# Prologue of a fused attention and feed-forward kernel: one denominator and one maximum operation, key-value transposes in the replica bank, and a reordered entry into the feed-forward steps

## The chip, the cores and the metric

The kernel runs on one core of one Trainium2 chip. The metric is the device time of one execution in microseconds (us). Five runs of the kernel before gave a median of 194.73 us, from 194.39 to 196.03.

The text uses the profile's names of the engines: PE is the matrix engine and PEld its weight loads, DVE the vector engine, ACT the scalar engine, POOL the GpSimd engine. SP is the engine that issues nearly all DMA transfers, in one queue and in program order. Each engine works through its own instructions in order, and semaphores hold an instruction until what it needs is there.

## The reference

The first half is attention with a polynomial feature map in place of the softmax, for batch 4, 4 heads, sequence 1088, head dimension 32. S1 and S2 are 8x32 matrices.

```python
def phi(x):
    a = np.einsum('rd,bhsd->bhsr', S1, x)
    b = np.einsum('rd,bhsd->bhsr', S2, x)
    return np.einsum('bhsi,bhsj->bhsij', a, b).reshape(*x.shape[:-1], r * r)
q_p, k_p = phi(q), phi(k)                        # 64 features
kv  = np.einsum('bhsf,bhsd->bhfd', k_p, v)
z   = np.sum(k_p, axis=2)
num = np.einsum('bhsf,bhfd->bhsd', q_p, kv)
den = np.einsum('bhsf,bhf->bhs', q_p, z)[..., None] + 1e-06
attn = num / den
```

The heads are then put side by side, which gives 4352 tokens of width 128, and the second half is a feed-forward layer on them: `h = max(x @ w_in, 0)`, then `out = (h * h) @ w_out`, with an inner width of 2048.

## The kernel before

**Tiling.** A batch has 1088 tokens. They are worked on in three chunks of 384, 384 and 320 tokens. The feed-forward layer of one chunk is 16 steps, one for each block of 128 inner columns. So there are 4 x 3 x 16 = 192 steps. A step is a first-layer matmul into `pg` (L908), a relu into `gt` by ACT (L918) or DVE (L920), a square into `g` by ACT (L902), DVE or POOL (L929), and a second-layer matmul that adds into `po` (L939). `ffn1(i)` records the first three, and `ffn2(i)` the last. The first layer runs three steps ahead (`LA = 3`). PSUM has two buffers for `pg`, so the first layer of step i+2 waits for the relu of step i.

**Prologue.** Before step 0 the attention of batch 0, chunk 0 must be there. Keys are turned on DVE (`a_kT`), PE makes their features `kf`, ACT and DVE build the products `kp`, and PE sums keys times values and keys alone over nine tiles of 128 tokens into `kvp` (L393, L407). The queries' features are made by three "replica" matmuls `rep` (L1087), each followed by a product on DVE (L1092). Two of the replicas stand in the two halves of `x0`, a PSUM tile of two banks in the pool slot named X. Then `nd` (L778) multiplies queries and sums into numerators and denominators in another tile, in the pool slot named N. `kvT` (L486) turns the sums for later chunks and writes into that same tile; `kw` (L498) copies the turned sums out.

The function `a_x1` takes denominators `den` (for chunk 0 by two ACT operations, L794) and row maxima `mx` (two DVE operations, L805, one for each bank), and a reciprocal `rden`. `a_x2` and `a_x3` scale the numerators to `xs` in 16 bits by a power of two that is taken off again after the layer. The squared power `beta` comes from two small DVE operations, `mp` and `beta` (L857, L861), at the end of `a_x3`. `a_xp` and `a_xT` turn `xs` into the layer's input `xT`. `keep_warm` runs matmuls on a tile of zeros while PE has nothing to do: `WARM0` of them at the start and `WARM` in front of step 0.

**What else runs beside the steps.** Chunk 1 of batch 0 (`old_chunk`) makes its query features on DVE by lane shuffles (`qb`, `qa`) and products (`qp`), and then needs an `nd` group of its own on PE. Chunk 2 makes them on PE (`a_qg`, L519) and DVE (`a_sh`). `br` holds `beta` spread over the partitions; `f_br` makes it by 16 small copies on POOL for each of the first two chunks, and `f_ob` multiplies a finished output chunk by it (L1003) before SP stores it (L1013). Batch 1 is prepared meanwhile: loads, `a_kT`, key features in a group with the `ndn` matmuls of chunk 2 (L550 with L431), their spreading `a_fs` (L352), the products `a_kp2` (L361, one half on DVE, one on POOL), and their sum over nine tiles, `a_kv9`. From batch 1 on, query features move between partitions by SP transfers, the `ft` moves (`a_mv`, L626).

**What sets the order.** The order is written out by the program. `_Plan` is a list of slots, one for each step. A task is added with its engine, a duration, the tasks that it needs and sometimes a first slot; it goes to the first slot in which that engine's planned load stays under a cap, one or two slots after what it needs. On POOL tasks take non-overlapping stretches. `balance()` then chooses for each step which engines do relu and square, from what the slots have left. The main loop records, for slot i, the first layer of step i+3, the second layer of step i and then that slot's tasks. DMA issues are in the plan too; in the program an issue on SP also waits for the landing of the DMA eight before it.

The entry into the steps is written by hand:

```python
    for cols in ((0, 128), (128, 384)):
        ffn1(0, ("ACT", "DVE"), cols)
    for i in range(1, LA):
        ffn1(i, ("ACT", ("DVE", "ACT")[i % 2]))
    a_qg(0, 2)
    for cols in ((0, 128), (128, 384)):
        ffn2(0, cols)
```

Of the kernel before, what the change touches and what calls it, by code (L numbers as in the profile page):

```python
# [73 lines left out]
def kernel(  # L74
# [26 lines left out]
    WARM0, WARM = 9, 7  # L101
# [61 lines left out]

    s_nat = cpool.tile([32, 32], F32)
# [3 lines left out]
    zero = cpool.tile([128, 512], F16)  # L168
    nc.vector.memset(zero[:], 0.0)  # L169
# [34 lines left out]
    load_qk(qn[0], q, 0, 384, 768)  # L204
    load_w_in(0, nc.sync)
    load_w_o(0)
    load_qk(qn[0], q, 0, 768, S)
# [20 lines left out]
    eps = cpool.tile([128, 1], F32)  # L228
    nc.gpsimd.memset(eps[:], 1e-6)
# [16 lines left out]
    def a_set(i):  # L246
        if i == 0:
            p_ = list(S2r.ap)[0][0]
            for g in range(2):
                nc.sync.dma_start(  # L250
                    bass.AP(S2r.tensor, S2r.offset + g * p_, [[2 * p_, 64], [1, 32]]),
                    bass.AP(S2.tensor, S2.offset, [[0, 8], [D, 8], [1, D]]),
                )
            nc.gpsimd.memset(sw[0][:], 0.0)
# [48 lines left out]
    for h in range(H):  # L303
        (nc.vector.tensor_copy if h < 2 else nc.scalar.copy)(
            _ap(sk, 32 * h, 32, 16 * h, [[1, 2], [2, 8]]),
            _ap(s_T, 0, 32, 0, [[8, 2], [1, 8]]),
        )
# [175 lines left out]
    def a_kvT(b):  # L483
        c0 = 768 if b == 0 else 512
        for i in range(2 if b == 0 else 1):
            nc.tensor.transpose(  # L486
                st[b, "N"][:, c0 + 128 * i : c0 + 128 * i + 128],
                st[b, "kvs"][:, 128 * i : 128 * i + 128],
                iden[:, :],
            )  # L490
        if b > 0:
            nc.tensor.matmul(st[b, "N"][:, 640:672], S2b[:, :], st[b, "gm"][:, :])

    def a_kw(b):

        n, c0 = (256, 768) if b == 0 else (128, 512)
        kw = st[b, "kw"] = wpool.tile([128, 256], F32, tag="kw", name="kw")
        nc.scalar.copy(kw[:, 0:n], st[b, "N"][:, c0 : c0 + n])  # L498
# [288 lines left out]
    def a_x1(b, ch):  # L787
# [4 lines left out]
        for g in range(2):  # L792
            if ch == 0:
                nc.scalar.activation(  # L794
                    _ap(den, 0, 128, 2 * g, [[4, 3], [1, 2]]),
                    _ap(nd, 0, 128, 512 * g + 32, [[66, 3], [33, 2]]), Iden, bias=eps[:, 0:1],
                )
        if ch > 0:
            nc.vector.tensor_scalar(
                out=_ap(den, 0, 128, 0, [[2, 2], [4, 3], [1, 2]]),  # L800
                in0=_ap(nd, 0, 128, 32, [[512, 2], [66, 3], [33, 2]]),
                scalar1=1e-6, scalar2=None, op0=add,
            )
        for g in (1, 0):
            nc.vector.tensor_reduce(  # L805
                out=_ap(mx, 0, 128, 2 * g, [[4, 3], [1, 2]]),
                in_=_ap(nd, 0, 128, 512 * g, [[66, 3], [33, 2], [1, 32]]),
                axis=AX, op=amax, apply_absolute_value=True,
            )
# [27 lines left out]
    def a_x3(b, ch, o=0, n=3):  # L837
# [17 lines left out]
        if o + n == 3:  # L855
            mp = wpool.tile([128, 3], F32, tag="mp", name="mp")
            nc.vector.tensor_scalar(  # L857
                out=mp[:, :].bitcast(U32), in0=mm[:, :].bitcast(U32),
                scalar1=EXP, scalar2=None, op0=band,
            )  # L860
            nc.vector.scalar_tensor_tensor(  # L861
                out=st[b, "beta"][:, 3 * ch : 3 * ch + 3], in0=mp[:, :], scalar=2.0**-20,
                in1=mp[:, :], op0=mult, op1=mult,
            )
# [194 lines left out]
    def keep_warm(n):  # L1059

        t_ = st["warm"]
        for _ in range(n):
            nc.tensor.matmul(t_[:, 0:512], zero[:, 0:128], zero[:, :])  # L1063
# [4 lines left out]
    a_fs(0, 0)  # L1068
    a_kf(0, 1, psf, "pg")
# [38 lines left out]
    for lo, n in ((0, 2), (2, 3)):  # L1108
# [6 lines left out]
    for t in range(4, NT):  # L1115
        st[0, "kp", t] = kp4, [256 * (t - 4) + 64 * h for h in range(H)]
    for t in range(4):
        a_kv(0, t)
        a_z(0, *st[0, "kp", t], False)
    x0 = psa.tile([128, 1024], F32, tag="X", name="rep")  # L1120
    replicated(0, x0[:, 0:512])
# [23 lines left out]
    products(1)  # L1145
    a_qT(0, 384, 768)
    a_kvs(0)
    a_nd(0, 0)
    a_kvT(0)
    a_qc(0, 1, psf, "po")  # L1150
# [12 lines left out]
    a_qb(0, 1)  # L1163
    a_qT(0, 768, S)
# [30 lines left out]
    def old_chunk():  # L1195

        b, ch = 0, 1
        P.at["qb", b, ch] = -1
        for e in range(E):
            P.add(("qa", b, ch, e), "DVE", 0.58, [("qb", b, ch)], a_qa, b, ch, e)  # L1200
# [5 lines left out]
        P.at["N"] = P.at["x3", b, ch]  # L1206
        P.add(("xd", b, ch), "SP", 0.0, [("x3", b, ch)], a_xd, b, ch)
# [60 lines left out]
    def x_tasks(b, ch):  # L1268
# [13 lines left out]
        if b == 0:  # L1282
            P.add(("xs", b, ch), "POOL", 0.95, [("rs", b, ch)], a_xs, b, ch)
# [3 lines left out]
        P.add(("bt", b, ch), "POOL", 1.0, [("s2", b, ch)], a_beta, b, ch)  # L1287
# [4 lines left out]
    def k_tasks(n):  # L1292
        for g in range(2):
# [7 lines left out]
        if n == 1:  # L1301
            x_tasks(0, 2)
# [27 lines left out]
    P.add(("kw", 0), "ACT", 0.4, [], a_kw, 0)  # L1330
    old_chunk()
    f_br(0, 0, 0, 1)
# [4 lines left out]
    P.add(("br", 0, 0), "POOL", 2.6, [], f_br, 0, 0, 1, 4)  # L1337
# [11 lines left out]
    P.add(("br", 0, 1), "POOL", 3.6, [("x3", 0, 1)], f_br, 0, 1)  # L1349
# [57 lines left out]
    for cols in ((0, 128), (128, 384)):  # L1407
        ffn1(0, ("ACT", "DVE"), cols)
    for i in range(1, LA):
        ffn1(i, ("ACT", ("DVE", "ACT")[i % 2]))  # L1410
    a_qg(0, 2)
    for cols in ((0, 128), (128, 384)):
        ffn2(0, cols)
# [49 lines left out]
```

## Time and profile before

| what | value |
|---|---|
| median of five runs | 194.73 us |
| the profiled execution, whole | 194.57 us |
| its span, first to last instruction | 192.8 us |
| PE busy | 184.5 us, 96% of the span |
| ACT, DVE, POOL busy | 68%, 61%, 47% of the span |
| first matmul of the feed-forward layer | starts at 16.90 us |
| first second-layer matmul | starts at 18.89 us |
| mean granted PE clock | 0.993 of full |

The profile is of one execution, and all its times count from the start of its span; some 1.8 us of the execution lie outside the span. A line of the profile gives a start or a total, a length, the engine, the line of the program and the operation with its tiles. "SPq" is SP's queue of issues. In the chain of waits, each piece is the work that the next one waited for, followed back from the last instruction. PE operations overlap their neighbours, so a matmul's own length is longer than the time from its start to the next one's.

### The profile page before, as it was taken

The page shows a single profiled execution, that of the slowest core. Times are in us where ns is not written, and L with a number is a line of the kernel's source. Part 1 is how long each engine was busy: PE and PEld are TensorE (multiplying, and loading weights), DVE is VectorE, ACT ScalarE, POOL GpSimd, SP SyncE. Part 2 cuts the span into 40 slices and gives each one's busy share as a digit, 9 for nine tenths or more (in the row PEclk, how much of TensorE's full clock was granted, in tenths as well). Part 3 has the DMA queues.
Part 4 walks back from the last instruction along what each step waited for, and adds up shares of the span by engine and source line. Part 5 has one row for each costly group of instructions (what it writes and reads, how often), then busy time and mean ns, then how long its engine had stood idle before and what let it go on. Part 6 is the DMA issues. An engine that isn't in the chain of part 4 may idle for free.

```text
span 192.8 us, 4421 instructions
## 1 busy us (share of the span) xinstructions
PE 184.5 (96%) x1540; PEld 110.1 (57%) x1540; DVE 118.5 (61%) x284; ACT 130.5 (68%) x322; POOL 90.4 (47%) x172
## 2 busy tenths in 40 slices
PE   7997999999999989999999999999999999999990
PEld 2673655474655456555556456555566555556990
DVE  3858995966739836466439764684382835637740
ACT  3316696956949848677769676587595966856840
POOL 5834465682447933334648941532666642250000
PEclk9999999999999999999999999999999999999997
DMA  5699406020143500341346201202304021200201
GB/s 164 155 299 318 91 20 236 0 44 0 40 93 87 169 10 24 66 119 35 69 96 180 60 0 37 51 2 58 47 12 85 12 58 27 41 0 2 44 0 36
DMA packets 30081, 13.93 MB, mean 72 GB/s; under 512 B 20202, under 2 KB 28778, under 8 KB 30058
## 3 DMA queue, kind: packets, MB, share of 16 engines
q1 hardware_dynamic: 29910, 13.58, 28.9%
q8 instruction: 12, 0.20, 0.4%
q14 instruction: 11, 0.09, 0.2%
q10 hardware_dynamic: 148, 0.07, 0.1%
HBM read 8.80 MB, written 2.23 MB: 57 GB/s over the span
## 4 chain that ended last, share of the span: by engine, by line
PE 81%; SPq 5%; DVE 5%; DMA 3%; issue 2%; ACT 1%; DVEq 0%; ACTq 0%
PE po L939 50%; PE pg L908 14%; PE kvp L393 3%; SPq L141 3%; PE ndn L637 2%; PE warm L1063 2%; PE pt L956 2%; DMA ft<-ft 2%; PE nd L778 2%; PE qk L564 1%; PE rep L1087 1%; SPq L626 1%; SPq L1013 1%; DMA ft<-u 1%; DVE kp L361 1%
## 5 line engine op out<-in xcount | busy, mean ns | idle before, releaser
L939 PE MATMUL po<-g,w_o 128*128 128x384 f32 (+3 forms) x386 | 144.1, 459 | 0.0
L918 ACT ACTIVATE gt<-pg 128x384 f32<-128x384 f32 (+2 forms) x139 | 65.3, 473 | 35.6 <-PE pg L908 35.0
L939 PEld LDWEIGHTS po<-g,w_o 128*128 128x128 f32 x386 | 65.6, 190 | 33.3 <-ACT g L902 16.9
L902 ACT ACTIVATE g<-gt 128x384 f32<-128x384 f32 (+1 forms) x146 | 72.2, 506 | 6.9 <-DVE gt L920 6.4
L908 PE MATMUL pg<-xT,w_in 128*128 128x384 f16 (+2 forms) x193 | 60.9, 317 | 0.7 <-ACT xT L880 0.3
L929 POOL TENSOR_TENSOR g<-gt 128x384 f32<-128x384 f32 (+1 forms) x44 | 34.8, 798 | 46.5 <-ACT gt L918 46.4
L920 DVE TENSOR_SCALAR gt<-pg 128x384 f32<-128x384 f32 (+1 forms) x54 | 28.8, 534 | 27.4 <-PE pg L908 20.0
L908 PEld LDWEIGHTS <-w_in 128*128 128x128 f16 x193 | 19.1, 99 | 22.1 <-issue 4.3
L599 POOL TENSOR_TENSOR qp<-tq,bs 128x384 f32<-128x384 f32 (+1 forms) x18 | 14.2, 811 | 16.1 <-DVE bs L591 16.1
L361 POOL TENSOR_TENSOR kp<-fs 128x384 f32<-128x384 f32 x9 | 13.2, 1488 | 1.3 <-DVE fs L352 1.3
L573 DVE STREAM_TRANSPOSE tq<-qk 128x384 f32<-128x384 f32 (+1 forms) x9 | 5.0, 561 | 13.0 <-PE qk L564 8.6
L738 POOL TENSOR_TENSOR bt<-s 128x384 f32<-128x384 f32 (+1 forms) x10 | 8.2, 815 | 7.1 <-DVE s L712 7.1
L971 POOL COPY br<-beta 32x3 f32<-32x3 f32 x32 | 5.8, 182 | 6.7 <-DVE beta L861 5.4
L985 DVE SCALAR_TENSOR_TENSOR sc<-po,bt 128x384 f32<-128x384 f32 (+1 forms) x9 | 4.8, 531 | 6.4 <-PE po L939 6.3
L361 DVE TENSOR_TENSOR kp<-fs 128x1152 f32<-128x1152 f32 x3 | 7.2, 2416 | 0.0
L720 DVE TENSOR_SCALAR rs<-ndn 128x384 uint32<-128x384 uint32 (+1 forms) x9 | 4.8, 536 | 3.6 <-PE ndn L704 3.5
L637 PE MATMUL ndn<-ft,kw 64*32 64x192 f32 (+1 forms) x144 | 6.4, 325 | 0.6 <-DMA ft<-u 0.6
L393 PEld LDWEIGHTS kvp<-kp,vn 128*32 128x32 f32 x288 | 5.4, 109 | 2.7 <-PE pg L908 1.1
L1063 PE MATMUL warm<-zero 128*128 128x512 f16 x16 | 5.7, 521 | 1.2 <-DVE zero L169 1.2
L325 DVE STREAM_TRANSPOSE qT<-qn 128x384 f32<-128x384 f32 (+1 forms) x12 | 6.5, 540 | 0.0
L393 PE MATMUL kvp<-kp,vn 128*32 128x64 f32 x288 | 6.5, 223 | 0.0
L637 PEld LDWEIGHTS ndn<-ft,kw 64*32 64x32 f32 x144 | 2.5, 104 | 5.9 <-PE pg L908 5.0
(147 smaller groups left out, 161.5 us busy)
## 6 DMA issues: line engine op xcount, KB each, us to landing
vn<-in_v_dram SPq DMA_DIRECT2D x32, 64.0 KB, 2.2
kn<-in_k_dram SPq DMA_DIRECT2D x3, 544.0 KB, 4.8
qn<-in_q_dram SPq DMA_DIRECT2D x3, 544.0 KB, 4.1
ft<-u SPq DMA_DIRECT2D x24, 48.0 KB, 1.9
out_dram<-oT SPq DMA_DIRECT2D x24, 48.0 KB, 1.8
w_in<-in_moe_w_in_dram SPq DMA_DIRECT2D x2, 512.0 KB, 7.3
w_o<-in_moe_w_out_dram SPq DMA_DIRECT2D x2, 512.0 KB, 8.6
ft<-ft SPq DMA_DIRECT2D x12, 48.0 KB, 2.0
```

Source lines behind the costliest of these rows:

```text
L361: (nc.vector if g == 0 else nc.gpsimd).tensor_tensor(out=_ap(st[b, "kp2"], 0, 128, 128 * (NT * g + lo), [[64, 2 * (hi - lo)], [8, 8], [1, ...
L393: nc.tensor.matmul(st[b, "kvp"][32 * h : 32 * h + 32, 0:64], _ap(vn[b], 0, n, v0 + dv * h, [[1, 32]]), kp[0:n, at[h] : at[h] + 64], start= ...
L599: nc.gpsimd.tensor_tensor(out=_ap(qp, 0, 128, 0, [[32, m], [8, 4], [1, 8]]), in0=_ap(st[b, "tq", ch], 0, 128, 4 * e, [[32, m], [1, 4], [0, ...
L637: nc.tensor.matmul(nd[32 * h : 32 * h + 32, 512 * g : 512 * g + n], st[b, "kw"][64 * g : 64 * g + 64, 32 * h : 32 * h + 32], st[b, ch, "ft ...
L738: nc.gpsimd.tensor_tensor(out=bt[:, 0:n], in0=st[b, "s2", ch][:, 0:n], in1=st[b, "s2", ch][:, 0:n], op=mult)
L902: nc.scalar.activation(dst, src, Square)
L908: nc.tensor.matmul(pg[:, c0:c1], w_in[:, 128 * c : 128 * c + 128], st[b, "xT"][:, 384 * ch + c0 : 384 * ch + c1],)
L918: nc.scalar.activation(gt[:, c0:c1], pg[:, c0:c1], Relu)
L920: nc.vector.tensor_scalar(out=gt[:, c0:c1], in0=pg[:, c0:c1], scalar1=0.0, scalar2=None, op0=amax)
L929: (nc.vector if on[1] == "DVE" else nc.gpsimd).tensor_tensor(out=g2[:, c0:c1], in0=gt[:, c0:c1], in1=gt[:, c0:c1], op=mult)
L939: nc.tensor.matmul(st["po", b, ch][:, c0:c1], w_o[:, 128 * c : 128 * c + 128], g2s[i][1][:, c0:c1], start=first, stop=(c == NFF - 1), skip ...
L1063: nc.tensor.matmul(t_[:, 0:512], zero[:, 0:128], zero[:, :])
```

## The change

- In `a_x1`, `den` is one DVE operation over both banks for chunk 0 too, and `mx` is one operation over both banks for both chunks. The two ACT operations and the tile `eps` are gone.
- `a_kvT` of batch 0 writes the turned sums into the first 256 columns of the replica tile `x0`, no longer into the tile of `nd`. `kw` follows at once on ACT, before the cast of the first half of `w_in`; it was a task of slot 0.
- `replicated(0, ...)` stands before the sums of the first four key tiles, no longer after them. `kp4` is made in parts of three and two tiles (it was two and three).
- The queries of batch 0 from column 384 on come in one load, no longer two, and both turns of them stand before `a_x1`.
- `mp` and `beta` become a function of their own, `a_bt`, planned in slot 1 for chunk 0 and behind `x3` for chunk 1.
- The entry: DVE and ACT take turns at relu and square from step 0's first part on, step 0's second layer starts before step 2's first layer, and `a_qg(0, 2)` stands behind step 2's first layer. `qb` of chunk 1 is a task of slot 0.
- `zero` has 128 columns, is filled first and is read four times over. `WARM` is 4, and one warm matmul stands between the two groups of `kf`. One copy of `sk` goes to ACT and one to POOL.
- The fills and sums of `sw` and `pr` on POOL become `a_set(2)` and stand before the steps.
- In the plan: `xs` and `bt` of chunk 2 on POOL get first slots 20 and 24; `br` of chunk 0 is one task of 16 copies that needs `bt`, in slot 6; `br` of chunk 1 gets first slot 20; `x_tasks(0, 2)` stands before the `fs` and `kp` tasks of batch 1.

As the plan comes out: the `nd` of chunk 1 goes from slot 3 to 4, the group of L550 and L431 from slot 10 to 11, POOL's `kp` of batch 1 from slots 12 to 14 to slots 15 to 17, `a_kv9` stays in slot 19, and `br` of chunk 1 goes from slot 20 to slot 30, behind `qp2` of batch 1. The POOL squares of steps 13 and 19 go to ACT; from slot 42 on the two plans are the same.

```diff
-    WARM0, WARM = 9, 7
+    WARM0, WARM = 9, 4
...
-    load_qk(qn[0], q, 0, 384, 768)
+    load_qk(qn[0], q, 0, 384, S)
     load_w_in(0, nc.sync)
     load_w_o(0)
-    load_qk(qn[0], q, 0, 768, S)
...
     def a_kvT(b):
-        c0 = 768 if b == 0 else 512
+        dst = st["kvT", b] = x0[:, 0:256] if b == 0 else st[b, "N"][:, 512:672]
...
-        for g in range(2):
-            if ch == 0:
-                nc.scalar.activation(
-                    _ap(den, 0, 128, 2 * g, [[4, 3], [1, 2]]),
-                    _ap(nd, 0, 128, 512 * g + 32, [[66, 3], [33, 2]]), Iden, bias=eps[:, 0:1],
-                )
-        if ch > 0:
-            nc.vector.tensor_scalar(
...
-        for g in (1, 0):
-            nc.vector.tensor_reduce(
-                out=_ap(mx, 0, 128, 2 * g, [[4, 3], [1, 2]]),
-                in_=_ap(nd, 0, 128, 512 * g, [[66, 3], [33, 2], [1, 32]]),
-                axis=AX, op=amax, apply_absolute_value=True,
-            )
+        nc.vector.tensor_scalar(
+            out=_ap(den, 0, 128, 0, [[2, 2], [4, 3], [1, 2]]),
+            in0=_ap(nd, 0, 128, 32, [[512, 2], [66, 3], [33, 2]]),
+            scalar1=1e-6, scalar2=None, op0=add,
+        )
+        nc.vector.tensor_reduce(
+            out=_ap(mx, 0, 128, 0, [[2, 2], [4, 3], [1, 2]]),
+            in_=_ap(nd, 0, 128, 0, [[512, 2], [66, 3], [33, 2], [1, 32]]),
+            axis=AX, op=amax, apply_absolute_value=True,
+        )
...
+    replicated(0, x0[:, 0:512])
     for t in range(4):
         a_kv(0, t)
         a_z(0, *st[0, "kp", t], False)
-    x0 = psa.tile([128, 1024], F32, tag="X", name="rep")
-    replicated(0, x0[:, 0:512])
...
+    a_set(2)
     a_qT(0, 384, 768)
+    a_qT(0, 768, S)
     a_kvs(0)
     a_nd(0, 0)
     a_kvT(0)
+    a_kw(0)
...
-    a_qb(0, 1)
-    a_qT(0, 768, S)
...
-    f_br(0, 0, 0, 1)
+    P.fix(("bt", 0, 0), "DVE", 0.35, 1, a_bt, 0, 0)
...
-    P.add(("br", 0, 0), "POOL", 2.6, [], f_br, 0, 0, 1, 4)
+    P.add(("br", 0, 0), "POOL", 3.6, [("bt", 0, 0)], f_br, 0, 0)
...
-    P.add(("br", 0, 1), "POOL", 3.6, [("x3", 0, 1)], f_br, 0, 1)
+    P.add(("br", 0, 1), "POOL", 3.6, [("bt", 0, 1)], f_br, 0, 1, first=20)
...
-    for cols in ((0, 128), (128, 384)):
-        ffn1(0, ("ACT", "DVE"), cols)
-    for i in range(1, LA):
-        ffn1(i, ("ACT", ("DVE", "ACT")[i % 2]))
+    ffn1(0, ("DVE", "ACT"), (0, 128))
+    square_due()
+    ffn1(0, ("ACT", "DVE"), (128, 384))
+    ffn1(1, ("DVE", "ACT"))
+    ffn2(0, (0, 128))
+    ffn1(2, ("ACT", "DVE"))
     a_qg(0, 2)
-    for cols in ((0, 128), (128, 384)):
-        ffn2(0, cols)
+    ffn2(0, (128, 384))
```

## The prediction

> **What bounds the kernel now.** First the shares, then the chain that ended last in order of time, then single instructions where that chain leaves the matmul engine. The page's shares:
>
> ```profile
> PE 184.5 (96%) x1540; PEld 110.1 (57%) x1540; DVE 118.5 (61%) x284; ACT 130.5 (68%) x322; POOL 90.4 (47%) x172
> ```
>
> PE is the bound. From 24 us on it repeats one step: 0.16 us first layer, 0.65 us second. So the change pays only by letting the steps start sooner, and loses where a later PE group waits. The chain of waits, each piece with start and length:
>
> ```profile
> 10.95 0.86 PE rep L1087 x2
> 11.88 1.56 PE nd L778 x24
> 13.44 0.38 PE nd L486 x2
> ...
> 13.91 0.43 ACT den L794 x2
> 14.37 0.62 DVE mx L805 x2
> 14.99 0.15 DVE rden L810
> ...
> 15.97 0.70 DVE xs L846 x3
> ...
> 17.46 0.28 PE pg L908
> 17.77 0.39 ACT gt L918
> 18.20 0.32 PE pg L908
> 18.52 0.43 PE qg L519 x16
> 18.96 0.85 PE po L939 x4
> ```
>
> Between nd's end, 13.44, and the first second-layer matmul, 18.96, the path runs over the two transposes (L486), ACT, nine DVE operations and ACT again: latency, not load. Step 1's second layer starts at 20.13. The chain leaves PE once more later:
>
> ```profile
> 50.74 0.59 DVE oT L979
> ...
> 53.46 0.54 SPq L1013
> ...
> 57.08 1.91 SPq L141
> ...
> 62.41 3.31 DMA ft<-ft
> ...
> 66.85 1.88 DMA ft<-u
> ```
>
> The left column is the start, the second the length, both in us. From 51.3 to 62.4 SP issues without a pause (the lines left out are its other stores and loads); behind that backlog the ft moves land late, and PE waits twice for them (0.34 and 0.30 us at 67.8 and 68.8). A delay of SP here delays PE one for one. That sets what a late br costs. POOL's work in time order:
>
> ```profile
> 39.93 3.53 POOL L971 COPY br<-beta 32x3 f32<-32x3 f32 x16
> ...
> 48.05 1.65 POOL L599 TENSOR_TENSOR qp<-tq,bs 128x384 f32<-128x384 f32 x2 [1.78 <-DVE bs L591]
> ```
>
> [...]the trace has 0.31 each at L805. [...]the 1152-wide kp took 2.80 and 2.22 us beside POOL's, and POOL's three took 2.99 and 5.09. [...]
>
> **The change, part by part.**
>
> *Start.* Durations are those of the one profiled execution. zero is filled first and a quarter as wide, so the warm matmuls start some 0.2 us earlier; one more stands inside the kf group. Nothing follows: kf4 needs kq (6.26), and rep needs qT, whose load let it begin at 6.21. The moved sk copies end by 4.81 as now; the added POOL copy (0.25) shifts sr, needed at 7.8, from 6.31 to 6.56.
>
> *Second replica early.* PE does rep2 and rep0 back to back, then all nine kv tiles. From 6.94: 0.88 + 0.84 + 1.03 + 1.10 = 10.79 against 10.95: PE's switch from replica to kv (0.25 for the first group instead of 0.11) is paid once instead of twice. The kp4 halves, now 3+2 tiles, are there at about 9.4 and 10.0; PE asks at 9.7 and 10.4. rep1 then ends 11.65, nd 13.28: **-0.16** (0 to -0.17).
>
> *den, mx, kvT.* den waits now for the transposes, which write nd's buffer (13.82 + 0.09); in the replica bank they don't hold it. After: semaphore 0.07, den 0.09 (24.06 to 24.15 at L799), one mx of 384: start to next start of the pair is 0.53, so 0.265 each[...]; one of double width 0.47[...]. rden follows nd's end by 0.63; now by 14.90 - 13.44 = 1.46. **-0.83.** Cover: both q transposes (0.47 + 0.50) are now ahead of den, 12.14 to 13.15, where DVE idled 1.49. They need the merged q load. Not waited for at 12.30 now, it carries 164 KB more; at 290 GB/s (w_in to w_out landings, 524 KB in 1.81 us) that is 0.56 us. I put its landing at 12.2; bounds 11 and 12.9, loss 0 to 0.6, taken 0. The queue order delays the first w_in and w_out by as much: w_in lands about 13.9 (its ACT cast now follows kw, at 14.1), w_out by 15.8 (15.25 at latest now), wanted at 16.8. SP issues one DMA fewer; in the program an issue waits for the landing of the DMA eight before it, and that pairing shifts by one: the first v load of batch 1 now waits for the merged q load, and the fifth for the second w_out as now (18.65).
>
> *First steps.* xs starts at 14.98. The last xT ends 16.43 and the second part of step 0 goes out at 16.47. DVE now does the small relu (16.16 to 16.40), before xT ends; ACT squares it by 16.7 and relus the large part to 17.15 (0.3 after its matmul's 0.28); DVE squares that to 17.5 and relus step 1 to 18.0. PE then does, each released in time: step 2's first layer 17.19, q features to 17.95 (0.43), rest of step 0's second layer, two first layers, step 1's second layer at **18.72**. That is 3.74 after xs against 4.16 now: **-0.42** (0 to -0.5). Of this, today's squares g of step 0 wait for DVE, busy with qb and qT up to 17.75; both have moved. So have mp and beta (two of 0.16): they feed br of chunk 0, wanted only by ob at slot 18. POOL fills and adds sw and pr right after the identities (11.5 now, then idle to 16.99), no longer at 18.44, so the second w_in casts come no later. kw leaves ACT's busy stretch at 20.40 for 13.75, in front of the w_in cast, which must end by 15.6 for the first xT: 14.1 + 1.04 does. Four warm matmuls end at 15.2, before xp at 15.37; seven would not.
>
> *Chunk 1's q features.* qb, both qa and both qp are DVE work after step 2's square, 18.6 to 21.7; nd goes one step later, at 21.8, and finds them. Now it waits 0.13 for qp. **-0.13.** With one step more done, nd ends at 23.29 where now it and that step would end at 24.83: together -1.54.
>
> *Later.* The qk group moves from slot 10 to 11; x is made before fs, and POOL's kp goes from slots 12-14 to 15-17, kv9 stays at 19. With the group's end as X: fs done X+2.2, POOL's kp at the slower 5.1 us plus a memset done X+7.5; the kv group begins X+6.63 and reaches its third kp at X+7.55. A tie: 0 to 0.5, **+0.1**. (fs: 1.85 us from dT to x in separate starts, begun 0.45 before X, and 0.85 for fs. The kv group has nine parts of 0.153 and waits for kp by thirds.) Steps 13 and 19 lose their POOL square, ACT carries 0.4 more beside ax; the square has some 0.45 of lead: **+0.05**.
>
> *br of chunk 1* moves from slot 20 to 30, behind qp2 (ends 49.70 in today's times): 49.70 + 3.53 = 53.23. ob, on DVE at 51.96 now, waits for it and ends 53.77; SP, today at 53.46 for its stores, goes at 53.82. Behind ob on DVE: kT, 54.4, and step 39's relu, 54.9, wanted at 54.58 by PE: 0.3, inside the same delay. Behind SP's stores, on the same queue: ten v loads and one q load of batch 2, the six ft moves of the next chunk, and PE waits for those. **+0.36** (0 to 0.4).
>
> Each later item counts in today's times, since PE sets the pace of the slots. Sum: -1.54 + 0.1 + 0.05 + 0.36 = **-1.0**. Span 192.8 to 191.8; the execution has 194.57, 1.8 around the span, so 193.6; the median of the runs is 0.16 above it: **193.7 us**. A difference under 0.5% (1.0 us) cannot be told from none.
>
> **Rivals.** *Nothing is given back:* POOL copies at their 182 ns busy time, br ends 52.6 before SP asks, kp in time. 194.7 - 1.5 = 193.2. For it: lead of 0.9 at SP today. Against: 16 copies took 3.53, not 2.9. *Given back downstream:* the early steps run behind ACT, whose relu and square together also need 0.81 per step[...]: -1.54 + 0.42 + 0.36 + 0.45 = -0.3, 194.4. *The q load comes late:* if the merged transfer needs the 7.3 us from issue to landing that w_in showed, it lands at 14.8, the transposes end 15.8, den starts 2.4 late: -1.5 + 2.4 + 0.36 = +1.2, **195.9**, slower. A landing at 13.4 eats the whole gain, one at 14.4 makes it slower by 0.5%; that the smaller load of now had landed by 12.30, 4.8 us after its issue at 7.52, speaks against it. *The change doesn't do what it says:* kvT still held by or holding nd; the program's waits show none, so it has no share.
>
> **Numbers.** Forecast 0.57 (193.2 to 194.2, just over half of it beyond 0.5%), nothing given back 0.20, given back 0.17, late load 0.06. Faster 0.57 x 0.55 + 0.20 = 0.52; slower 0.07, with a little for a clock drop; the rest 0.41. Range 192.9 to 194.9.
>
> **What would show it.** rden starts at 13.9, 0.6 after nd's end; ACT has kw ahead of its w_in cast; step 1's second layer near 18.7, nd of chunk 1 without a wait. br ends after 53 in today's times, and SP's stores follow ob at once; PE waits about 1 us for ft before its second such group. Wrong if DVE sits waiting for qn, [...]if PE idles at the kv group, or if br is early.

## The result, and the profile after

The changed kernel took 194.27 us in the median, beside 194.65 us for the kernel before on the same chip: ratio 0.996, 95% interval 0.9941 to 0.998, which is 0.8 us faster (0.4 to 1.15). A second set gave 194.13 us and 0.998 (0.9946 to 1.0014). The prediction was 193.7 us and 1.0 us faster, with a range of 192.9 to 194.9. So the time lies within the range, 0.6 us above the likeliest value, and the gain is at the edge of what can be told from none. The medians here are over all executions, while ratios and intervals leave out those more than 1.5% above the fastest of their kernel, 10 of 36 of the changed kernel and 10 of 15 in the experiment fetch_nd.

The profiled execution took 194.31 us (194.57 before), its span is 192.5 us (192.8). The page's shares after:

```profile
PE 183.8 (95%) x1538; PEld 110.0 (57%) x1538; DVE 117.3 (61%) x284; ACT 131.1 (68%) x322; POOL 88.1 (46%) x168
```

The chain of waits after, from the last replica on (start, length, engine, line; times in us):

```profile
10.50 0.86 PE rep L1083 x2
11.36 0.07 issue
11.43 1.57 PE nd L776 x24
13.00 0.02 issue
13.02 0.17 DVE den L790
13.20 0.46 DVE mx L795
13.66 0.15 DVE rden L800
...
14.64 0.70 DVE xs L836 x3
15.34 0.04 issue
15.39 0.23 PE xp L863
15.62 0.25 issue
15.87 0.23 PE xp L863
...
16.55 0.43 PE pg L900 x2
16.98 0.38 PE po L931 x2
17.36 0.26 PE pg L900
17.61 0.43 PE qg L517 x16
18.04 0.63 PE po L931 x2
18.67 0.33 PE pg L900 x2
19.00 0.69 PE po L931 x2
```

The transposes and both ACT operations have left the chain between nd and rden. A piece of 0.25 us before the third xp is new, and nothing that the profile shows ends it. Step 1's second layer starts at 19.00, where the kernel before had 20.13. Later in the same chain stand the two places at which PE waits for the ft moves:

```profile
60.78 3.53 DMA ft<-ft
...
65.42 1.88 DMA ft<-u
...
102.85 4.68 DMA ft<-ft
...
107.59 1.84 DMA ft<-u
109.42 0.14 issue
109.56 0.97 PE ndn L635 x10
```

POOL's work in time order, where br of chunk 1 now stands:

```profile
46.97 1.65 POOL L597 TENSOR_TENSOR qp<-tq,bs 128x384 f32<-128x384 f32 x2 [3.86 <-DVE bs L589]
48.56 3.54 POOL L963 COPY br<-beta 32x3 f32<-32x3 f32 x16
```

The two profiles can be laid side by side, since PE does the same steps. The table gives nd's end, the time from there to step 1's second layer, and how far a step's first-layer matmul starts from that of the same step in the kernel before (minus is earlier), for steps near 31, 65, 70, 111 and 138 us. It holds the experiments too, all but fetch_nd. The places at which a column changes are the places at which something was won or lost.

| kernel | nd ends | to step 1's second layer | at 31 | at 65 | at 70 | at 111 | at 138 |
|---|---|---|---|---|---|---|---|
| before | 13.44 | 6.69 | 0 | 0 | 0 | 0 | 0 |
| after | 13.00 | 6.00 | -1.25 | -0.99 | -1.42 | -0.54 | -0.45 |
| again (after, once more) | 13.80 | 5.72 | -0.72 | -0.45 | -0.95 | -1.35 | -1.66 |
| den_alone | 13.85 | 5.99 | -0.44 | -0.41 | -0.39 | +0.48 | +0.18 |
| den_warm4 | 13.24 | 5.81 | -1.22 | -1.21 | -1.65 | -0.79 | -1.09 |
| undo_entry | 13.12 | 6.58 | -0.58 | -0.32 | -0.26 | +0.30 | +0.24 |
| br_early | 12.85 | 5.59 | -1.74 | -1.60 | -2.22 | -1.29 | -1.59 |
| before_qlate | 13.89 | 6.70 | +0.45 | +0.45 | -0.98 | -1.43 | -1.74 |
| qload_late | 13.59 | 5.58 | -1.07 | -0.81 | -2.25 | -2.55 | -2.85 |
| kvT_back | 13.07 | 6.36 | -0.81 | -0.53 | -1.97 | -1.90 | -2.20 |
| br_qlate | 13.23 | 6.15 | -0.65 | -0.51 | -1.94 | -2.38 | -2.68 |
| shift_br_qlate | 13.32 | 6.56 | -0.41 | -0.25 | -1.68 | -2.13 | -2.43 |
| q_split | 13.75 | 5.75 | -0.52 | -0.39 | -1.83 | -2.24 | -2.51 |

Two things are read off at once. nd's end differs by up to 1 us between kernels that are the same up to there, since the loads land at different times (the first keys at 3.51 in one profile, the second at 5.91 in another) and, where PE's own early matmuls decide, since these take different times (the first `kf` group 0.63 us in one, 1.03 in another); so a profile's own start says little, and the column beside it is the one that measures the prologue. And where the changed kernel stood 0.99 us ahead at 65 us, just what the prediction's sum says, it won 0.43 between 65 and 70 us and lost 0.88 between 70 and 111 us, where the two programs are the same. What sets these two changes is shown below, with the late q loads. The experiments ask what each part of the prologue gave, and what happens at those two places.

### The profile page after: what moved, and what is told of

Read it like the earlier page. It is cut to its first block, busy times and chain, and to the rows that moved or that the text cites. A ratio compares the mean times of both kernels' runs of the same rounds, so it can differ in the third digit from the quotient of the medians.

```text
span 192.5 us, 4411 instructions
## 1 busy us (share of the span) xinstructions
PE 183.8 (95%) x1538; PEld 110.0 (57%) x1538; DVE 117.3 (61%) x284; ACT 131.1 (68%) x322; POOL 88.1 (46%) x168
## 4 chain that ended last, share of the span: by engine, by line
PE 75%; DMA 8%; DVE 7%; POOL 4%; issue 3%; ACT 0%; SPq 0%; POOLq 0%; ACTq 0%
PE po L931 46%; PE pg L900 13%; DMA ft<-ft 4%; PE ndn L635 3%; PE kvp L391 2%; DMA ft<-u 2%; PE pt L948 2%; PE qk L562 2%; PE nd L776 2%; POOL br L963 1%; DMA kn<-in_k_dram 1%; PE rep L1083 1%; POOL kp L359 1%; POOL qp L597 1%; DVE fs L350 1%
## 5 line engine op out<-in xcount | busy, mean ns | idle before, releaser
L910 ACT ACTIVATE gt<-pg 128x384 f32<-128x384 f32 (+2 forms) x136 | 63.9, 473 | 34.5 <-PE pg L900 34.0
L894 ACT ACTIVATE g<-gt 128x384 f32<-128x384 f32 (+2 forms) x151 | 74.2, 503 | 7.1 <-DVE gt L912 6.5
L921 POOL TENSOR_TENSOR g<-gt 128x384 f32<-128x384 f32 (+1 forms) x40 | 31.2, 786 | 42.4 <-ACT gt L910 42.2
L912 DVE TENSOR_SCALAR gt<-pg 128x384 f32<-128x384 f32 (+2 forms) x57 | 29.9, 527 | 26.2 <-PE pg L900 20.8
L359 POOL TENSOR_TENSOR kp<-fs 128x384 f32<-128x384 f32 x9 | 15.1, 1707 | 5.3 <-DVE fs L350 5.2
L359 DVE TENSOR_TENSOR kp<-fs 128x1152 f32<-128x1152 f32 x3 | 6.7, 2222 | 0.0
L1055 PE MATMUL warm<-zero 128*128 128x512 f16 x13 | 4.8, 530 | 1.0 <-DVE s_nat L167 1.0
```

The lines of the kernel that those rows point to most:

```text
L359: (nc.vector if g == 0 else nc.gpsimd).tensor_tensor(out=_ap(st[b, "kp2"], 0, 128, 128 * (NT * g + lo), [[64, 2 * (hi - lo)], [8, 8], [1, ...
L894: nc.scalar.activation(dst, src, Square)
L910: nc.scalar.activation(gt[:, c0:c1], pg[:, c0:c1], Relu)
L912: nc.vector.tensor_scalar(out=gt[:, c0:c1], in0=pg[:, c0:c1], scalar1=0.0, scalar2=None, op0=amax)
L921: (nc.vector if on[1] == "DVE" else nc.gpsimd).tensor_tensor(out=g2[:, c0:c1], in0=gt[:, c0:c1], in1=gt[:, c0:c1], op=mult)
```

## The experiments

**The same kernel again.** No edit.

> The changed kernel once more, for the landing of the ft moves near 103 us. In its first profile the steps ran 1.43 us ahead of the kernel before up to there, and 0.54 after it, since the first ft move of batch 2's second chunk took 4.68 us to land and PE waited 0.67 us at 109.56. Theory A (the landing differs from execution to execution): another profile has another length there, by over 0.5 us, and the steps after 110 us run 0.9 to 1.4 ahead. Theory B (the early steps put the move behind the batch's q load, 1.36 us after its issue): the same 4.7 us within 0.3 and the same 0.5 ahead. Either way the ratio to the kernel before is 0.996, within 0.002.

Ratio 0.998 (0.9946 to 1.0014). At 111 us it was 1.35 us ahead, not 0.54: in this profile PE did not wait there. SP's waits for a transfer between 98 and 112 us (total, times, longest, in us), in the changed kernel's first profile:

```profile
SPq L624 <- DMA ft<-ft: 2.3, 1, 2.3
```

And in this one:

```profile
SPq L624 <- DMA ft<-ft: 0.3, 1, 0.3
```

The same program waits 2.3 us or 0.3 us for the same move. Theory A holds for the size, and the ratio lies within the 0.002 that was expected; from this run alone it can't be said what the move waits for.

**den, mx, kvT and kw alone.** The kernel before with this part of the diff (`a_kvT`, `a_kw` and `a_x1` as changed, `a_kw(0)` behind `a_kvT(0)`), and then with four warm matmuls for seven.

```diff
-    WARM0, WARM = 9, 7
+    WARM0, WARM = 9, 4
```

> The kernel before with only one den, one mx, kvT in the replica tile and kw right behind it. By the prediction's step: xs starts 0.83 us earlier, at 15.14 for 15.97, all steps follow, and nothing is given back later, since br, kp and the entry stay: 0.83 us faster, ratio 0.9957. Rival (the first steps run behind DVE's and ACT's other work of that stretch, qb, the second q turn, w_in's cast, which do not move): xs is as early, but step 1's second layer comes less than 0.5 us earlier than 20.13, and the ratio is above 0.998.

> The kernel before with the den, mx, kvT and kw part, and four warm matmuls for seven. With seven, PE came to its first xp only at 16.37, while the first xs was there by about 15.8: nd end to step 1's second layer took 5.99 us (6.69 before). Theory (seven warm matmuls hold back what the shorter chain won, as the prediction said): 5.6 to 5.8. Rival (DVE's qb and second q turn, in front of step 0's squares, hold it anyway): 5.9 to 6.0. The ratio is 0.9955 in the first case and 0.9965 in the second, too near to tell by itself.

With seven warm matmuls nd to step 1's second layer took 5.99 us for 6.69, with four 5.81, at the edge of the 5.6 to 5.8 that was expected. The chain of the second:

```profile
11.68 1.57 PE nd L778 x24
...
13.27 0.17 DVE den L792
...
15.63 0.30 PE xp L863 x2
...
19.05 0.65 PE po L931 x2
```

From nd's end, the steps at 31 us are 0.85 and 1.02 us earlier than in the kernel before (column "at 31" less the difference in nd's end), and they keep it to 65 us. By the same measure three profiles with the whole change, which lost little to what is described below, gave 1.08 to 1.22 (again, br_early, qload_late), so this one part, of some ten in the change, with the four warm matmuls brings most of it. Seven warm matmuls ran to 16.37, past the first xs, as the prediction had said; four are done before xp. The seven of the kernel before took 1.67 us, from 14.29 on, and its first nine 4.02, from 1.23 on: 0.22 and 0.42 us from start to start, at a granted clock of 1.00 for both. Why the early ones are slower, no run shows. The times can't tell these two kernels apart from the changed one: 0.9996 (0.9962 to 1.0029), which leaves out the 0.9957 that was expected, and 0.9927 (0.9888 to 0.9966), from 7 executions, which takes in both of its expected values. Both lost 0.86 to 0.87 us between 70 and 111 us, as the changed kernel did in its first profile.

**kvT back in nd's tile**, with the late q loads of the next experiment:

```diff
-        dst = st["kvT", b] = x0[:, 0:256] if b == 0 else st[b, "N"][:, 512:672]
+        dst = st["kvT", b] = st[b, "N"][:, 768:1024] if b == 0 else st[b, "N"][:, 512:672]
```

> The changed kernel with the late q loads, and kvT back in nd's tile (its columns 768 to 1024), the one den and one mx kept. The prediction's step: den then waits for the two transposes, and starts 0.40 to 0.47 us after nd's end (0.47 in the kernel before) for 0.02; all that follows is late by the same: nd end to step 1's second layer 6.0 us for the 5.58 of the kernel with the late q loads alone, ratio 0.9907 for 0.9886. Rival (one DVE operation for two of ACT is the whole gain, and the transposes' columns don't hold it): den 0.02 after nd's end, 5.6 to 5.7 us, ratio unchanged.

The chain of waits of this kernel, from nd to den:

```profile
11.51 1.56 PE nd L776 x24
13.07 0.38 PE nd L484 x2
13.45 0.02 issue
13.47 0.38 ACT kw L496
13.85 0.02 issue
13.88 0.17 DVE den L790
```

den starts 0.81 us after nd's end for 0.02, and all behind it is 0.78 us late (6.36 for 5.58). That den is held is as predicted, the size is not: the chain has kw between the transposes and den, since kw now reads the shared tile right away, and den starts behind that read. Ratio 0.995 (0.9922 to 0.9978), 0.9886 without this edit. From nd's end to rden it is 1.44 us here, beside 1.55 in the kernel before and 0.66 with the other tile. Some 0.40 of the 1.44 is kw, which in the kernel before came later, so by an estimate from this chain the one DVE operation would be worth about 0.5 us with the transposes in nd's tile and kw in its old place; no run shows that kernel.

**The old entry.** The changed kernel with the entry's order of before.

> The changed kernel with the entry in its old order (relu on ACT and square on DVE for both parts of step 0, step 2's first layer ahead of step 0's second layer), all else as changed. The prediction put 0.42 us on the first steps, the new order among them: then step 1's second layer starts up to 0.42 us later than 19.00, and the ratio is 0.998. Rival (from the two profiles: xs start to step 1's second layer took 4.36 us after and 4.16 before, so the new order brought nothing): 19.00 within 0.15, ratio 0.996.

Step 1's second layer started at 19.70, 6.58 us after nd. Of this, 0.62 is a stall of PE before the third xp, of which more below; without it 5.96, to 5.58 to 5.72 in the three profiles of the new entry (again, br_early, qload_late) where stall and slowed square, of which more below too, come to 0.15 us or less each. By this subtraction, from one profile, the new order brings 0.25 to 0.4 us: neither theory's number as it was put (19.00 within 0.15, or 19.42), and the direction of the prediction. The times can't show so little: ratio 0.9994 (0.9967 to 1.0021), beside 0.998 for the changed kernel in the same set of runs.

**The q load behind the moves.** Batches 2 and 3 get their 544 KB of queries in one load on SP's queue, right ahead of the six ft moves of 48 KB each. This edit puts it right behind them, in the changed kernel and in the kernel before.

```diff
-            at = 2 * i if n == 1 else s0 - 16 if i == 0 else s0 + 1 + 2 * i
+            at = 2 * i if n == 1 else s0 - 16 if i == 0 else s0 + 14 if i == 4 else s0 + 1 + 2 * i
```

> The changed kernel with the q load of batches 2 and 3 issued five slots later (slots 46 and 94), behind the six ft moves of slots 44 to 45 and 91 to 92. Theory B (the q load of 544 KB, issued 1.36 us ahead of the first ft move, holds that move's landing): the first ft move lands in about 2 us for 4.68, PE's waits for ft at 67 and at 109.6 us (0.2 and 0.67) go, and the kernel is 0.6 to 0.9 us faster than the changed one: ratio to the kernel before 0.992. Theory A (the landing differs by itself): the ratio stays at 0.996, and the wait at 109.6 is between 0 and 0.7 as it falls out.

> The kernel before with only the q loads of batches 2 and 3 moved behind the six ft moves (slots 46 and 94). Theory (the change's gain is that of the prologue alone, and what came later in the profiles is the ft moves behind the q load, in both kernels): PE's two waits for ft at 67.8 and 68.8 go. Against the changed kernel with this edit, whose steps ran 1.44 us further ahead of the kernel before from the group at 67 to 69 us on, then 0.30 at 111 and 0.30 at 138, the kernel before should gain these same 2.0 us: ratio 0.990, and the changed kernel with the edit (0.9886) stays ahead by what the prologue gives, 0.7 to 1.1 us in the steps before 60 us. Rival (the kernel before loses no more than its named waits, 0.64 us): ratio 0.9965, and the changed kernel's late q load gains by its earlier phase.

The changed kernel with it took 192.28 us, ratio 0.9886 (0.9856 to 0.9916), a larger gain than the 0.992 of theory B; the kernel before 192.96 us, ratio 0.994 (0.9916 to 0.9965), between the theory's 0.990, which the interval leaves out, and the rival's 0.9965. The waits of PE in the first, all that are left:

```profile
PE warm L1055 <- DVE s_nat L167: 1.0, 1, 1.0
PE pg L900 <- ACT xT L872: 0.3, 1, 0.3
PE xp L863 <- DVE xs L836: 0.2, 1, 0.2
```

and SP's issues near 102 us in time order:

```profile
102.02 1.15 SPq L624 DMA_DIRECT2D ft<-ft  x2
103.27 3.39 SPq L624 DMA_DIRECT2D ft<-u  x4
106.70 0.58 SPq L131 DMA_DIRECT2D qn<-in_q_dram  x1
```

No engine waits for an ft move any more, SP neither. The kernel before gained 1.43 us at 65 to 70 us, 0.45 by 111 and 0.31 by 138, 2.2 in its profile; 1.4 at the first place where the rival gave 0.64. The named waits are the smaller part of that loss: from the start of the group of ndn and qk matmuls to the next first layer PE needs 1.70 us in "again", with 0.28 us of named wait, and 0.76 here. Half of these 0.94 us lie between the eighth and the ninth matmul of the group, 0.61 us from start to start for 0.14; the profile names 0.28 of it, since it counts from the modelled end of the matmul before. In the other half the matmuls follow each other more slowly.

With the load in front, the landing of the first ft move alone sets where PE stands behind it. At the first place it landed 1.41, 0.93, 0.38, 1.66, 0.25 and 2.21 us before that of the kernel before (65.72) in after, again, den_alone, den_warm4, undo_entry and br_early, and the column "at 70" has 1.42, 0.95, 0.39, 1.65, 0.26 and 2.22. At the second place, in the five of them whose chain runs over the move, it landed between 106.76 and 108.59, and the column "at 111" follows it within 0.06 us. So what the changed kernel won and lost there came from when SP issued that move and how long it took to land (3.25 to 3.58 us, then 4.36 to 4.72), and from where the steps stood only as far as that moved SP. Theory A was right on how the loss varies, theory B on what causes it. The chains give an ft move behind the 544 KB 3.25 to 4.72 us to land, and with the load behind it, it kept nobody waiting. Whether it is the order in one queue, or that load and moves share the DMA engines at all, no run separates: the load was not tried on another queue. Between the two kernels with this edit the ratio is 0.9886 / 0.994 = 0.9946, or 1.05 us for the change (0.3 to 1.8 by both intervals, from two sets of runs); the profiles give 1.11 at 138 us, of which 0.30 is that nd ended earlier.

**br of chunk 1 early**, alone and with the late q loads:

```diff
-    P.add(("br", 0, 1), "POOL", 3.6, [("bt", 0, 1)], f_br, 0, 1, first=20)
+    P.add(("br", 0, 1), "POOL", 3.6, [("bt", 0, 1)], f_br, 0, 1)
```

> The changed kernel with br of chunk 1 without its first slot: it goes from slot 30 to slot 10, where POOL is free, and ob no longer waits for it; POOL gets three squares back (steps 37, 41, 42). The prediction's step (br in slot 30 costs 0.36): PE's loss of 0.25 at slot 38 goes, SP's stores of the chunk are issued 0.3 to 0.4 us earlier, and with them the v loads and ft moves, so that PE's wait for ft at 67 shrinks by up to 0.3: ratio 0.993 to 0.995. Rival (the ft moves' landing hangs on the q load in front of them, not on SP's issue): only the 0.25 at slot 38, ratio 0.9948, and the wait at 67 us as before within 0.15.

> The changed kernel with both edits: br of chunk 1 in slot 10, q loads of batches 2 and 3 behind the ft moves. With the ft waits gone, PE alone sets the pace from 60 us on, so what br costs at slot 38 shows in the end undiminished: 0.25 us less than with the late q load alone, ratio 0.9873 (0.9886 less 0.0013). Rival (a POOL square put back makes its step late, or SP's earlier issue changes nothing): 0.9886 or above.

POOL then does both br in one row, before kp (br_early; 31 of the 32 copies, the first of which began at 23.75):

```profile
23.97 6.93 POOL L963 COPY br<-beta 32x3 f32<-32x3 f32 x31
32.62 3.87 POOL L359 TENSOR_TENSOR kp<-fs 128x384 f32<-128x384 f32 x2 [1.72 <-DVE fs L350]
```

The loss of 0.25 us at slot 38 is gone in both kernels (their lead doesn't change from 40 to 65 us); by 65 us it had shrunk to 0.10 in the changed one. SP's stores of that chunk went out at 51.86, 1.60 us before those of the kernel before, just as its steps; in the changed kernel only 0.74 before, at a lead of 1.09. That is the predicted delay of 0.36, at 0.35. It did not reach the ft moves: SP's four stores took 1.89 us for 2.08, its eight v loads 4.54 for 4.68, which gives 0.33 back. The v loads took 4.44 to 5.23 us in the seven profiles with the old place of the q loads, with and without a late br, so how much they give back differs from one profile to the next. Times: 0.9948 (0.9919 to 0.9977) alone, which fits the prediction's step and the rival alike, and 0.9872 (0.9832 to 0.9912) with the late q loads, whose own is 0.9886: as expected in the middle, and not to be told apart from it.

**PE's instruction stream.** In three of eight profiles with the changed prologue and its order of PE work, PE stood before the third xp, for 0.25, 0.62 and 0.26 us (after, undo_entry, br_qlate). A single packet on the queue that the page calls "instruction" came 2.0 to 2.3 us after nd's start in these three, and 1.0 to 1.8 in the other five; each stall ended 2.35 to 2.47 us after the packet. In "again" the third xp began 0.14 us later than it otherwise follows the second, within the second one's length, and 2.41 us after its packet; in the other four it began without delay, 2.58 to 3.44 us after it. So in none of the eight did it begin sooner than 2.35 us after the packet. To test this, the early warm matmuls were cut up, so that more PE instructions stand ahead, at the same work:

```diff
-    keep_warm(WARM0)
+    keep_warm(3)
+    for _ in range(24):
+        nc.tensor.matmul(st["warm"][:, 0:128], zero[:, :], zero[:, :])
```

> The changed kernel with the late q loads, and with six of the nine early warm matmuls (512 columns) cut into 24 of 128 columns, so that 36 more PE instructions stand ahead of nd, at the same warm work. In three of six profiles of the new prologue PE stood 0.25 to 0.62 us at its third xp, at nothing that the profile names, until 2.35 to 2.55 us after a single packet on the queue for instructions; in the other three that packet came earlier, or the third xp later. Theory (PE stands at a place in its instruction stream until the next part of the stream has been brought in): the place moves 36 instructions up, into nd, where PE otherwise has no pause: nd takes longer than 1.57 us, with idle time of 0.3 us or more that is put down to nothing, and the third xp never waits; ratio above that of the late q loads alone by 0.001 to 0.006. Rival (the stall belongs to the third xp, for xs, PSUM or another release that the profile misses): nd takes 1.57 us, and the third xp waits 0 to 0.6 us as before.

> Late q loads, br of chunk 1 in slot 10, and two of the nine early warm matmuls cut into eight of 128 columns: 12 more PE instructions ahead of the steps. Theory of the instruction stream: the place moves from the third xp to the first warm matmul in front of the xps, whose work is filler, so the third xp no longer waits: nd end to step 1's second layer 5.6 to 5.7 us (6.15 with both edits and the stall of 0.26), and with br's 0.1 to 0.25 us the fastest of all: ratio 0.985 to 0.988. Rival: the third xp waits in half of the executions as before, and the ratio is that of the two edits, 0.9872 or above.

The chain of the first:

```profile
11.94 1.19 PE nd L776 x17
13.12 3.49 issue
16.61 1.06 PE nd L776 x7
```

PE stood 3.49 us in the middle of nd, until 2.5 us after the packet (14.1), and the third xp no longer waited. This is one profile; the execution took 196.77 us, and the median of the kernel's 15 was 196.22. Then the table by stretch of the same kernel (PE, PEld, DVE, ACT and POOL busy, granted clock, DMA share, GB/s):

```profile
13.00:16.50 3.50, 0.12 (x3) 0.00 (x0) 0.33 (x1) 0.00 (x0) 0.55 (x3) 1.00 1.08 337
16.50:18.00 1.50, 1.39 (x9) 1.27 (x10) 0.29 (x2) 0.00 (x0) 0.38 (x1) 0.57 1.12 357
18.00:20.00 2.00, 2.00 (x6) 0.87 (x5) 1.83 (x9) 1.32 (x2) 1.05 (x3) 0.50 0.93 184
20.00:22.00 2.00, 1.76 (x9) 0.63 (x7) 0.41 (x2) 0.88 (x4) 0.00 (x0) 0.97 0.39 99
```

The granted clock was 1.00 in the pause, 0.57 in the 1.5 us behind it, 0.50 in the next 2 us and 0.97 in the 2 us after. By an estimate from these means it stood at half for 3.4 us (16.7 to 20.1). In qload_late, which has no such pause, it was 1.00 from 11 to 22 us. Ratio 0.9992 (0.9944 to 1.0039) for 0.9886 with the matmuls whole, from the 5 shortest of the 15: it leaves out most of the cost. With 12 more instructions for 36 the pause moved to the warm matmuls, as expected:

```profile
14.33 1.13 issue
15.46 1.02 PE warm L1055 x4
```

It ended 2.36 us after the packet (13.1). But it was not hidden there: the four warm matmuls came after the pause and held the xps until 16.3, and nd to step 1's second layer took 6.56, not 5.6. The expectation had the place right and the cost wrong. Ratio 0.988 (0.9832 to 0.9929), from 6 executions.

**The query load split again**, on top of br_qlate:

```diff
-    load_qk(qn[0], q, 0, 384, S)
+    load_qk(qn[0], q, 0, 384, 768)
     load_w_in(0, nc.sync)
     load_w_o(0)
+    load_qk(qn[0], q, 0, 768, S)
```

> Late q loads, br of chunk 1 in slot 10, and the query load of batch 0 in two parts again, in the old places of the queue, with the turn of its second part behind xT, where DVE idles 0.85 us in the changed kernel. In eight profiles of the new prologue with the same instruction count the packet on the instruction queue came 0.98 to 2.25 us after nd's start, in four of the old one 1.04 before to 0.1 after it. Theory (the merged load, ahead of 2 MB of weights, delays that packet): it comes within 0.5 us of nd's start or before, the third xp doesn't wait, nd end to step 1's second layer is 5.6 to 5.7 us, ratio 0.984 to 0.988. Rival (the packet is late for another reason, such as where PE stands in its stream): 1.0 to 2.3 after nd's start, and a stall of 0 to 0.6 us at the third xp in about half of the executions; or the second part lands too late for its turn, and the features of chunk 2 wait: ratio 0.987 to 0.992.

The packet came 1.03 us after nd's start: the rival, though this profile has no stall. So splitting the load did not bring the packet to where the old prologue has it, within 0.2 us of nd's start or before; one profile says no more, and what delays the packet stays open. (The 0.98 to 2.25 us of the expectation come from seven profiles, and are 1.06 to 2.33 when the packet's start is read exactly.) Ratio 0.991 (0.9884 to 0.9937). Both this kernel and br_qlate lost 0.2 to 0.3 us at another place: step 0's large square on DVE took 0.80 to 0.82 us for 0.43, when POOL's cast had begun just before it. The cast and the square in br_qlate, from the timelines of POOL and of DVE (start, length, what was done):

```profile
17.41 0.61 POOL L202 CAST w_in<-w_in 128x512 f16<-128x512 f32 x1 [4.03 <-DMA w_in<-in_moe_w_in_dram]
...
17.50 0.80 DVE L921 TENSOR_TENSOR g<-gt 128x256 f32<-128x256 f32 x1 [0.80 <-ACT gt L910]
```

The same two in qload_late, where the square begins first:

```profile
17.44 0.43 DVE L921 TENSOR_TENSOR g<-gt 128x256 f32<-128x256 f32 x1 [0.73 <-ACT gt L910]
...
17.47 0.87 POOL L202 CAST w_in<-w_in 128x512 f16<-128x512 f32 x1
```

Whichever begins first keeps its length, the other is longer by 0.26 to 0.39 us. What makes the later one wait, the traces don't name, and it is not longer by the full overlap. In br_qlate the square begins 0.52 us before the cast's end and is longer by 0.37; in qload_late the cast begins 0.40 us before the square's end and is longer by 0.26. In nine such overlaps of 0.21 to 0.54 us with the cast first (in after, again, br_early, br_qlate, q_split, the kernel before and before_qlate) and in four with the square first, the later one is longer by 0.14 to 0.15 us less than the overlap; one small square in undo_entry had 0.11.

## Why the prediction was right, and where it was not

*Second replica early, -0.16.* From the first replica of the chain to nd's end: 6.50 us before, and 6.50 to 6.52 in the kernels with the old order; 6.34 after, 6.14 to 6.33 in the others with the new one whose chain starts there. Right, and somewhat more in most profiles. In undo_entry it was 6.56: the second replica waited until 7.56 for POOL's copies of sr. The prediction has these done at 6.56, but the last two ran beside DVE's kp, took 0.66 and 0.58 us for 0.20 and ended at 7.51.

*den, mx, kvT, -0.83.* From nd's end to rden the chains give 1.55 us before and 0.66 after, 0.89 less. mx took 0.46 to the next start for the prediction's 0.47, which was the author's estimate and not shown by the trace before. The 0.31 us that the prediction gives for each mx of before is half of two operations that overlap: one took 0.36, and 0.27 to the next start, and the one of double width took 0.55. den_alone and den_warm4 show that this part carries most of the gain, kvT_back that with kw right behind the transposes the other tile is worth 0.78 of it. The merged q load was there in time in the profiles: both turns ran on at once behind the last product. The first half of w_in landed at 12.9 (issued at 7.71, 5.2 us to landing), a microsecond before the 13.9 that the prediction put for it. The rival of the late load fell.

*First steps, -0.42.* This step failed in its size. From the start of xs to step 1's second layer: 4.16 us before, 3.94 to 3.95 at best (br_early, qload_late, kvT_back), not 3.74. The order went as written, but the large part of step 0's second layer with two first layers took 0.96 us for the 0.77 of the sum. And it is not always had: 4.36 after, with PE's stall of 0.25, and 4.51 in br_qlate, with stall and slowed square. The stall is a cost that the prediction doesn't have; the profile of the kernel before shows none.

*Chunk 1's q features, -0.13.* nd of chunk 1 found its features. Together with the steps above 1.54 was predicted; measured from the first replica on it is 0.16 + 0.80 = 0.96 in the first profile, and in again, br_early and qload_late, with 1.08 to 1.22 from nd's end on, 1.25 to 1.6. That the first profile stood 1.25 us ahead all the same is the luck of its start: its replicas began 0.28 us earlier.

*Later.* kv9's tie: PE lost 0.12 to 0.17 us in every kernel with the new plan, none in den_warm4 with the old one; 0.1 was predicted. *br of chunk 1, +0.36*: br's end, ob behind it, SP 0.35 late and step 39's relu late all came as put. The step failed at its last link, that a delay of SP passes to the ft moves one for one: SP's next issues took 0.33 us less, and the cost was 0.25 at slot 38 and 0.10 by 65 us.

*The sum.* At 65 us the errors cancelled, which is luck: -1.25 + 0.15 + 0.11 = -0.99, where -1.0 was forecast. What followed was in no step: the ft moves stand behind a q load in both kernels, and what that costs near 110 us differs from execution to execution (0.05 us in again, 1.33 after, against the kernel before with the late load). The prediction took the waits of before as a base that stays. The rival "given back downstream" is nearer to the two measured gains, 0.8 and 0.4 us, than the forecast, but by this and not by its own reason: ACT's and POOL's early steps gave back nothing that shows, and a loss at kp, for which its sum has 0.45, was 0.12 to 0.17. Whether the changed kernel loses more at the moves than the kernel before in the mean is not settled: five profiles with an earlier prologue lost 0.56 to 0.93 us more there than the one of the kernel before, "again" 0.40 less; the change seems worth 1.05 us with the q load out of the way and 0.4 to 0.8 with it, and the intervals overlap.

The best kernels combine the change with the late q loads: 192.3 to 192.4 us, 2.1 to 2.2 us under the kernel before in the medians (qload_late, br_qlate). br early and the split load on top of it make no difference that these runs can tell.

## What to carry to other kernels

When a small operation starts late behind a producer, look at who else writes or reads its tile: with the two transposes back in that tile, and the copy that reads them right behind, the small operation started 0.79 us later, more than any other single part was seen to bring. A small transfer that an engine waits for should not stand behind a large one on the same queue, even where the waits that the profile names are short: 48 KB behind 544 KB took up to 4.72 us to land, and with the order turned no engine waited for them. And lay the two kernels' steps side by side before believing a sum of steps: a gain of 1 us in the first 20 us can be there in full, and a transfer 45 or 90 us later can still replace it by its own landing time (0.99 us ahead at 65 us, 1.42 at 70, 0.54 at 111).

## What the runs showed of the hardware that was not expected

- PE can stand still at a fixed place in its instruction stream until 2.35 to 2.50 us after one packet on the instruction queue: 0.25 to 3.49 us here, in the profile only as "issue". That it is this packet that ends the wait is inferred from these times and from the moved place. Adding 12 or 36 instructions ahead of the place moved it up. When the packet comes varies by 1.3 us against PE's work, and why is open.
- A matmul group whose operands came late took 0.94 us more than the same group undisturbed, with only 0.28 us of wait that the profile names; from start to start one gap of 0.61 us shows more of it.
- Where a square on DVE and a cast on POOL overlapped, the later one alone was longer, by 0.14 to 0.15 us less than the overlap, in 13 of 14 overlaps of 0.15 to 0.56 us.
- The same 48 KB move, issued 1.36 us after a 544 KB load in the same program, held SP for 2.3 us in one execution and for 0.3 us in another.
